# A written-out order of steps, changed: first roots on two engines, block weights and bias sooner, later units placed anew

## The chip, the cores and the metric

The kernel runs on one core of a Trainium2 chip. A core has a matrix engine (TensorE, PE in the profile, with its weight loads shown apart as PEld), a vector engine (VectorE, DVE), a scalar engine (ScalarE, ACT), GpSimd (POOL) and a queue engine for transfers (SyncE, SP). They run side by side, each through its own list of instructions in order, and wait for each other by counters (semaphores). The metric is the device time of one execution in microseconds (us); less is better.

## The reference

The input `x` has 2048 tokens of 512 numbers (bf16). Both halves start from the same layer norm, and their sum is added to `x`:

```python
xn = _layernorm(x, axis=-1)
return x + _A_ref(xn, A_wqkv, A_w_phi, A_wo) + _B_ref(xn, B_w1, B_b1, B_w2)
```

`_A_ref` is linear attention with 32 heads of 16: queries and keys are multiplied by a 16x16 matrix per head (`w_phi`), a softmax over the 16 is taken of the result and of its negative, and these 32 features replace the exponential kernel of attention:

```python
phi_k = jnp.concatenate([_softmax(pk, axis=-1), _softmax(-pk, axis=-1)], axis=-1)
kv = jnp.einsum("bhsf,bhsd->bhfd", phi_k, v)
num = jnp.einsum("bhqf,bhfd->bhqd", phi_q, kv)
den = jnp.einsum("bhqf,bhf->bhq", phi_q, z)[..., None] + 1e-6
```

`_B_ref` is a two-layer network with 1792 hidden units, a bias `b1` and the activation mish, `h * tanh(softplus(h))`.

## The kernel before, in words

The 2048 tokens are 16 tiles of 128, in four groups of four. The order of all the work is written out by hand in the string `STEPS` (line 24): one short name for one step, with its numbers, `@b` for the bank of PSUM (0 to 5) that it uses, and `a`, `v` or `p` for the engine that does it (ScalarE, VectorE, GpSimd). A loop at line 649 calls the functions in that order, and the table `run` (line 628) says which function a name stands for. There is no scheduler behind it: each engine gets its instructions in the order in which the steps stand. The waits between engines are put in by the framework, from which instruction reads or writes which buffer, in that same order.

The steps that matter here:

- `LS i`, `RS i`, `AZ i`, `TP i`, `TC i` (lines 550 to 589): moments of tile `i` of the first group, its root (one over the square root of variance plus epsilon), the centring, the transposition on TensorE (`ptr`), and the copy out of PSUM. `RS i a` is `Ln` and `Exp` on ScalarE (lines 558 and 559); `RS i p` is an addition and a power on GpSimd (lines 171 and 172).
- `TW`, `TK`, `WB`, `F0`, `FD`: key weights turned on TensorE (`ptw`), copied, multiplied by the block-diagonal matrix `Wbd` that `WB` makes of `w_phi` (`pfold`), and copied to `wkp`. `PB` and `CB` turn the bias and copy it to `b1f`. `KM` makes a mask that is used late.
- `LP i`: logits of the keys of the first two tiles (line 204). `L s i` and `LC s i`: logits of slot `s`, tile `i` (slots 0 to 3 are the keys of the four groups, 4 to 7 the queries), and their copy to SBUF by `take` (line 247). `V`, `VC`: values and their copy.
- `WL 1`, `WL 2` (`wide`, line 619): the logits of tiles 1 and 2 of the second group, not in a bank of the six but in a tile of two banks of their own, `pwide`, one half each. Their copies are `LC 1 1` and `LC 1 2`:

```python
wide_of[0] = ps2.tile([P, 2, 512], FP32, name="pwide", tag="kv")
pl_of[1, i] = project(wkp, TPG + i, wide_of[0][:, i - 1, :])
```

- `H u`, `M u`: a hidden unit, that is 128 hidden numbers for 512 tokens, as four matmuls (`ph`, line 223), and its mish on ScalarE (line 234), which also adds the bias.
- `E s`, `X s k`, `S s k`, `R s k`, `N s k`: the softmax of a slot: extremes on VectorE, exponentials on ScalarE (line 283), sums on VectorE (line 300), inverses and normalisation. `A`: the keys' products with the values.
- `LN g`, `AP g k`: layer norm of a later group, with a transposition by transfer. `DX`, `DW`, `WT`: loads on SP.
- From `KV` on: `W`, `Q`, `G`, `C` are the attention of the queries, `O` the second layer, `P` the projection, `Y` the residual and the store.

Mish and the exponentials need different tables on ScalarE. Whenever the kind of function changes, `table` (line 135) loads one (line 139).

Of the kernel before, what the change touches and what calls it, by code (L numbers as in the profile page):

```python
# [21 lines left out]

WARM, SHORT = 8, 0
STEPS = """
LS 0; LS 1; TW 0 @0; DX 2; TK 0 a; AW; TW 1 @1; RS 0 p; KM; WB; AZ 0; RS 1 p; AZ 1; F0 0 @2; TK 1 a;
FD 0 a; TP 0 @3; PB @4; TP 1 @5; TC 1 a; F0 1 @0; F0 2 @1; FD 2 a; TC 0 v; F0 3 @3; CB; FD 1 v; FD 3
a; LP i @4,2; LS 2; V 1 @5; LS 3; RS 2 a; AZ 2; TP 2 @0; RS 3 a; AZ 3; V 0 @1; LC 0 0 a; LC 0 1 a;
AM; TC 2 v; VC 1 a; TP 3 @3; TC 3 v; L 0 2 @4; LC 0 2 a; H 0 @0; M 0; L 0 3 @2; LC 0 3 a; LN 1; H 1
@3; E 0 0; M 1; H 2 @5; H 3 @4; H 4 @0; H 5 @2; M 2; M 3; M 4; AP 1 0; H 6 @3; AP 1 1; E 0 1; H 7
@5; LN 2; H 8 @4; H 9 @0; M 5; VC 0 a; M 6; M 7; H 10 @2; H 11 @1; H 12 @3; M 8; DX 3; WL 1; M 9; X  # L30
0 1; X 0 0; L 1 0 @5; L 1 3 @4; M 10; LC 1 0 v; LC 1 3 v; H 13 @0; H 14 @5; WL 2; M 11; M 12; M 13;
V 6 @4; LC 1 1 a; H 15 @2; H 16 @1; M 14; H 17 @3; H 18 @0; M 15; M 16; M 17; H 19 @5; M 18; M 19;
LN 3; S 0 1; LC 1 2 a; AP 2 0; AP 2 1; H 20 @2; H 21 @1; H 22 @3; M 20; M 21; M 22; H 23 @0; M 23;
VC 6 a; AP 3 0; AP 3 1; H 24 @5; M 24; H 25 @2; M 25; H 26 @1; H 27 @3; H 28 @0; M 26; H 29 @4; S 0
0; L 2 3 @5; M 27; M 28; M 29; E 1 0; L 2 0 @2; E 1 1; LC 2 0 v; L 2 2 @1; LC 2 2 v; L 3 2 @3; WT; R
0 0 a; LC 2 3 a; F 0 @0; L 2 1 @4; N 0 0; F 1 @2; F 2 @5; X 1 0; FC 2 a; L 3 0 @1; LC 3 0 a; FC 1 a;
LC 2 1 v; V 3 @4; FC 0 a; LC 3 2 v; V 4 @5; F 3 @3; FC 3 a; V 7 @1; V 2 @2; X 1 1; A 0 0; E 2 0; L 4
0 @0; VC 3 a; E 2 1; L 4 2 @3; L 3 1 @4; VC 2 a; R 0 1 a; VC 4 a; LC 4 0 a; S 1 1; N 0 1; L 3 3 @2;
L 4 3 @5; L 4 1 @0; VC 7 a; LC 3 3 a; LC 4 2 a; V 9 @1; LC 4 3 v; V 5 @2; S 1 0; X 2 0; VC 5 a; V 8
@3; R 1 1 a; VC 9 a; LC 3 1 a; N 1 1; VC 8 v; A 0 1; V 11 @5; VC 11 v; R 1 0 a; N 1 0; LC 4 1 a; H  # L40
30 @2; M 30; H 31 @1; M 31; H 32 @4; H 33 @3; H 34 @0; M 32; M 33; H 35 @5; M 34; M 35; H 36 @2; H
37 @1; H 38 @4; H 39 @3; M 36; M 37; M 38; M 39; DW 2; H 40 @0; H 41 @5; H 42 @2; E 3 0; M 40; M 41;
M 42; H 43 @1; A 1 0; S 2 0; M 43; A 1 1; DW 3; R 2 0 a; E 3 1; L 5 0 @4; X 2 1; L 6 2 @3; E 4 0; LC
5 0 a; L 5 3 @0; LC 5 3 a; E 4 1; V 14 @5; O 0 @2; VC 14 v; V 13 @1; X 3 0; X 3 1; V 10 @4; N 2 0;
VC 13 a; V 12 @5; VC 12 a; L 6 0 @0; VC 10 a; S 2 1; S 3 1; V 15 @1; R 2 1 a; N 2 1; L 6 1 @5; S 3
0; L 5 2 @4; LC 6 0 a; VC 15 a; X 4 0; LC 5 2 a; LC 6 2 a; O 1 @0; L 5 1 @1; LC 6 1 v; L 6 3 @4; H
44 @3; H 45 @5; S 4 0; A 2 0; R 3 0 a; N 3 0; LC 5 1 a; R 3 1 a; N 3 1; LC 6 3 a; H 46 @1; A 2 1; A
3 0; X 4 1; W 4 0 v; S 4 1; M 44; H 47 @4; M 45; A 3 1; M 46; M 47; H 48 @3; H 49 @5; M 48; H 50 @1;
H 51 @4; KV; M 49; W 4 1 v; M 50; E 5 0; E 5 1; M 51; H 52 @3; M 52; Q 0 0; G 0 0; H 53 @5; H 54 @1;
L 7 0 @4; Q 0 1; M 53; H 55 @3; L 7 3 @5; M 54; G 0 1; Q 1 0; O 2 @1; C 0 a; G 1 0; LC 7 0 a; LC 7 3  # L50
a; Q 1 1; L 7 1 @4; E 6 0; X 5 0; S 5 0; G 1 1; C 1 a; W 5 0 v; O 3 @5; LC 7 1 a; O 4 @4; E 6 1; M
55; P 0; Y 0; P 1; Y 1; O 5 @3; X 5 1; Q 2 0; P 2; L 7 2 @2; P 3; S 5 1; G 2 0; Q 2 1; Y 2; W 5 1 a;
O 6 @0; O 7 @1; LC 7 2 a; G 2 1; E 7 0; C 2 a; X 6 0; S 6 0; X 6 1; Y 3; W 6 0 a; Q 3 0; O 8 @2; P
4; G 3 0; Q 3 1; E 7 1; G 3 1; X 7 0; Y 4; P 5; O 9 @5; Q 4 0; S 6 1; O 10 @4; C 3 a; W 6 1 a; G 4
0; Q 4 1; G 4 1; Y 5; S 7 0; C 4 a; O 11 @3; X 7 1; W 7 0 v; Q 5 0; P 6; Y 6; P 7; G 5 0; S 7 1; Q 5
1; G 5 1; C 5 a; O 12 @0; W 7 1 a; Q 6 0; Y 7; P 8; P 9; Y 8; G 6 0; Q 6 1; O 13 @1; G 6 1; Q 7 0; G
7 0; P 10; P 11; Q 7 1; C 6 v; O 14 @2; Y 9; G 7 1; Y 10; P 12; P 13; OH 0 @5; Y 11; C 7 a; P 14; PH
0; OH 1 @4; Y 12; Y 13; Y 14; YH 0; PH 1; YH 1
"""


# [620 lines left out]
```

## Time and profile before

| | |
|---|---|
| median of 3 runs | 174.02 us (173.9 to 174.33) |
| profiled execution | 173.64 us, of it 171.9 us span from the first instruction to the last |
| PE busy | 167.7 us, 98% of the span |
| DVE busy | 142.2 us, 83% |
| ACT busy | 125.3 us, 73% |
| POOL busy | 7.8 us, 5% |
| mean granted TensorE clock | 0.998 |

The span leaves out 1.74 us of the profiled execution. The profile gives each engine's busy time, the chain of waits that ended last, groups of equal instructions by line, and a timeline: start and duration in us, engine, line, operation, what it writes and reads, how many alike were put together, and in brackets how long the engine had been idle and what ended that. Starts on one engine can lie up to 0.1 us ahead of the end of the instruction before, since they overlap. A matmul's duration includes its way through the array: those of 512 columns have 0.379 us in the profile and follow each other every 0.216 us (eight of them take 1.89 us).

### The profile page before, as it was taken

The page shows a single profiled execution, that of the slowest core. Times are in us where ns is not written, and L with a number is a line of the kernel's source. Part 1 is how long each engine was busy: PE and PEld are TensorE (multiplying, and loading weights), DVE is VectorE, ACT ScalarE, POOL GpSimd, SP SyncE. Part 2 cuts the span into 40 slices and gives each one's busy share as a digit, 9 for nine tenths or more (in the row PEclk, how much of TensorE's full clock was granted, in tenths as well). Part 3 has the DMA queues.
Part 4 walks back from the last instruction along what each step waited for, and adds up shares of the span by engine and source line. Part 5 has one row for each costly group of instructions (what it writes and reads, how often), then busy time and mean ns, then how long its engine had stood idle before and what let it go on. Part 6 is the DMA issues. An engine that isn't in the chain of part 4 may idle for free.

```text
span 171.9 us, 2729 instructions
## 1 busy us (share of the span) xinstructions
PE 167.7 (98%) x1044; PEld 82.4 (48%) x1044; DVE 142.2 (83%) x220; ACT 125.3 (73%) x204; POOL 7.8 (5%) x23
## 2 busy tenths in 40 slices
PE   8899999999999999999999999999999999999993
PEld 2554444444455454454444744544444444554452
DVE  2859998999599999989999998699789987875333
ACT  2788899988989899789897988996286275532200
POOL 4302102200000000000000000000000000000000
PEclk9999999999999999999999999999999999999999
DMA  5997280099960000000000254209345628768631
GB/s 139 273 377 256 43 203 0 2 183 209 302 225 0 0 4 0 0 0 4 0 0 0 59 99 91 56 7 156 92 113 104 149 58 192 153 135 199 155 96 61
DMA packets 44201, 18.02 MB, mean 105 GB/s; under 512 B 35996, under 2 KB 44188, under 8 KB 44188
## 3 DMA queue, kind: packets, MB, share of 16 engines
q1 hardware_dynamic: 43344, 17.60, 42.0%
q10 hardware_dynamic: 844, 0.25, 0.6%
q8 instruction: 8, 0.13, 0.3%
q14 instruction: 5, 0.04, 0.1%
HBM read 7.10 MB, written 2.10 MB: 53 GB/s over the span
## 4 chain that ended last, share of the span: by engine, by line
PE 95%; DMA 1%; POOL 1%; DVE 1%; issue 0%
PE po L457 28%; PE ph L223 28%; PE pl L189 14%; PE po L464 8%; PE pv L189 8%; PE pnd L412 2%; PE pkv L381 2%; DMA x_sb<-in_A_x_dram 1%; PE pl L204 1%; PE pwide L189 1%; PE pfold L151 1%; POOL rstd L172 1%; PE ptr L570 0%; DVE stats L165 0%; POOL rstd L171 0%
## 5 line engine op out<-in xcount | busy, mean ns | idle before, releaser
L457 PE MATMUL po<-w_sb,acts 128*128 128x512 bf16 (+2 forms) x238 | 50.8, 366 | 0.0
L223 PE MATMUL ph<-xnT,w_sb 128*128 128x512 bf16 x224 | 50.1, 379 | 0.0
L234 ACT ACTIVATE acts<-ph,b1f 128x512 bf16<-128x512 f32 x56 | 36.8, 694 | 4.7 <-PE ph L223 4.3
L300 DVE TENSOR_REDUCE s<-e 128x128 f32<-128x2048 bf16 x16 | 36.4, 2276 | 0.0
L457 PEld LDWEIGHTS <-acts 128*128 128x128 bf16 x238 | 22.2, 98 | 24.1
L223 PEld LDWEIGHTS <-w_sb 128*128 128x128 bf16 x224 | 21.6, 98 | 25.2
L283 ACT ACTIVATE e<-e 128x2048 bf16<-128x2048 bf16 x16 | 30.3, 1910 | 0.0
L189 PEld LDWEIGHTS <-xnT 128*128 128x128 bf16 x184 | 17.5, 98 | 19.6 <-DMA wv<-in_A_wqkv_dram 0.2
L471 DVE TENSOR_TENSOR x_sb<-po,x_sb 128x512 bf16<-128x512 f32 (+2 forms) x17 | 11.0, 656 | 8.8 <-PE po L464 8.8
L427 ACT COPY ds<-pnd 128x32 f32<-128x32 f32 x16 | 3.0, 185 | 18.3 <-PE pnd L412 18.3
L464 PE MATMUL po<-wqk,xnT 128*128 128x512 bf16 (+2 forms) x68 | 15.6, 366 | 0.0
L189 PE MATMUL pv<-wv,xnT 128*128 128x512 bf16 x64 | 15.4, 379 | 0.0
L189 PE MATMUL pl<-wqk,xnT 128*128 128x512 bf16 x64 | 15.4, 379 | 0.0
L247 ACT CAST p_sb<-pl 128x512 bf16<-128x512 f32 x22 | 12.3, 583 | 1.9 <-PE pl L189 1.9
L165 DVE BATCH_NORM_STATS2 stats<-x_sb 128x6 f32<-128x512 bf16 x16 | 10.1, 678 | 4.1 <-DMA x_sb<-in_A_x_dram 4.1
L139 ACT ACT_TABLE_LOAD x10 | 12.8, 1283 | 0.2
L258 DVE TENSOR_TENSOR m<-m 128x512 bf16<-128x512 bf16 (+1 forms) x32 | 11.5, 359 | 1.1
L189 PE MATMUL pl<-wkp,xnT 128*128 128x512 bf16 x48 | 11.5, 379 | 0.0
L258 DVE TENSOR_TENSOR m<-p_sb 128x1024 bf16<-128x1024 bf16 x16 | 10.9, 682 | 0.0
L267 DVE TENSOR_TENSOR e<-p_sb,m 128x2048 bf16<-128x2048 bf16 x8 | 9.8, 1225 | 0.9 <-PE pkv L381 0.7
L334 DVE TENSOR_TENSOR e<-e,r 128x2048 bf16<-128x2048 bf16 x8 | 9.7, 1218 | 0.7 <-ACT r L309 0.7
L267 DVE TENSOR_TENSOR e<-m,p_sb 128x2048 bf16<-128x2048 bf16 x8 | 9.8, 1225 | 0.3
(67 smaller groups left out, 133.5 us busy)
## 6 DMA issues: line engine op xcount, KB each, us to landing
w_sb<-in_B_w_dram SPq DMA_DIRECT2D x4, 896.0 KB, 7.3
out_dram<-x_sb SPq DMA_DIRECT2D x15, 128.0 KB, 2.0
x_sb<-in_A_x_dram SPq DMA_DIRECT2D x3, 512.0 KB, 7.8
wv<-in_A_wqkv_dram SPq DMA_DIRECT2D x1, 512.0 KB, 4.9
wqk<-in_A_wo_dram SPq DMA_DIRECT2D x1, 512.0 KB, 9.7
x_sb<-in_A_x_dram SPq DMA_DIRECT2D x2, 128.0 KB, 2.4
x_sb<-in_A_x_dram SPq DMA_DIRECT2D x1, 256.0 KB, 3.9
qT<-e SPq DMA_TRANSPOSE x16, 2.8
```

Source lines behind the costliest of these rows:

```text
L139: nc.scalar.preload_act_table_set(name)
L189: nc.tensor.matmul(pp, lhsT=xnT[:, t, kt, :], rhs=w[:, kt, :], start=(kt == 0), stop=(kt == KT - 1),)
L223: nc.tensor.matmul(ph_of[u][:], lhsT=w1_sb[:, kt, f * P : (f + 1) * P], rhs=xnT[:, g * TPG : (g + 1) * TPG, kt, :], start=(kt == 0), stop= ...
L234: nc.scalar.activation(acts[:, f, g * 512 : (g + 1) * 512], ph_of.pop(u)[:], ACT.Mish, bias=b1f[:, f : f + 1])
L247: copy(p_of[s][:, i, :], pl_of.pop((s, i)))
L258: nc.vector.tensor_tensor(out=m[:], in0=src[:, :, 0:half], in1=src[:, :, half : 2 * half], op=op)
L267: nc.vector.tensor_tensor(out=e_of[s][:].rearrange("p t j l c -> p (t j) l c")[:, :, pl, :].rearrange("p t (c e o) -> p t c e o", e=8, o=2 ...
L283: nc.scalar.activation(v, v, ACT.Exp)
L300: nc.vector.reduce_sum(t[:], pair(s, k).rearrange("p t j l (c e) -> p (t j l c) e", e=16), axis=AX.X)
L457: nc.tensor.matmul(po_of[t, c.stop][:, c], lhsT=acts[:, f, t * P : (t + 1) * P], rhs=w2_sb[:, f, c], start=(f == 0), stop=False,)
L464: nc.tensor.matmul(po_of[t, c.stop][:, c], lhsT=oT_of[t // 2][:, t % 2 * 4 + j, :], rhs=wo_sb[:, j, c], start=False, stop=(j == 3),)
L471: nc.vector.tensor_tensor(out=y, in0=po_of.pop((t, c.stop))[:, c], in1=y, op=ALU.add)
```

## The change

Only `STEPS` is changed; the steps are the same, in another order and with other banks and, for some copies, inverses and roots, on another engine. In the first group, `RS 0` goes from GpSimd to ScalarE and `RS 3` from ScalarE to GpSimd; `WB` and `PB` stand sooner, `KM` later. Behind that the order of nearly everything differs somewhat. The core of the diff, cut to the first half of the order:

```diff
-LS 0; LS 1; TW 0 @0; DX 2; TK 0 a; AW; TW 1 @1; RS 0 p; KM; WB; AZ 0; RS 1 p; AZ 1; F0 0 @2; TK 1 a;
-FD 0 a; TP 0 @3; PB @4; TP 1 @5; TC 1 a; F0 1 @0; F0 2 @1; FD 2 a; TC 0 v; F0 3 @3; CB; FD 1 v; FD 3
-a; LP i @4,2; LS 2; V 1 @5; LS 3; RS 2 a; AZ 2; TP 2 @0; RS 3 a; AZ 3; V 0 @1; LC 0 0 a; LC 0 1 a;
-AM; TC 2 v; VC 1 a; TP 3 @3; TC 3 v; L 0 2 @4; LC 0 2 a; H 0 @0; M 0; L 0 3 @2; LC 0 3 a; LN 1; H 1
-@3; E 0 0; M 1; H 2 @5; H 3 @4; H 4 @0; H 5 @2; M 2; M 3; M 4; AP 1 0; H 6 @3; AP 1 1; E 0 1; H 7
-@5; LN 2; H 8 @4; H 9 @0; M 5; VC 0 a; M 6; M 7; H 10 @2; H 11 @1; H 12 @3; M 8; DX 3; WL 1; M 9; X
-0 1; X 0 0; L 1 0 @5; L 1 3 @4; M 10; LC 1 0 v; LC 1 3 v; H 13 @0; H 14 @5; WL 2; M 11; M 12; M 13;
-V 6 @4; LC 1 1 a; H 15 @2; H 16 @1; M 14; H 17 @3; H 18 @0; M 15; M 16; M 17; H 19 @5; M 18; M 19;
-LN 3; S 0 1; LC 1 2 a; AP 2 0; AP 2 1; H 20 @2; H 21 @1; H 22 @3; M 20; M 21; M 22; H 23 @0; M 23;
...
+LS 0; LS 1; RS 0 a; TW 0 @0; RS 1 p; WB; AW; TW 1 @1; AZ 0; PB @2; TK 0 a; F0 0 @3; AZ 1; TK 1 a;
+CB; FD 0 a; TP 0 @4; TP 1 @5; F0 1 @0; F0 2 @2; TC 0 v; TC 1 a; KM; FD 2 a; F0 3 @1; FD 3 a; FD 1 v;
+LP i @4,3; LS 2; RS 2 a; LS 3; RS 3 p; V 1 @5; AM; AZ 2; TP 2 @0; TC 2 a; V 0 @2; LC 0 0 a; LC 0 1
+v; AZ 3; TP 3 @1; TC 3 v; L 0 2 @3; L 0 3 @0; LC 0 2 a; H 0 @4; LN 1; LC 0 3 a; DX 2; E 0 0; M 0; AP
+1 0; AP 1 1; VC 1 a; E 0 1; LN 2; H 1 @1; H 2 @3; M 1; M 2; H 3 @0; M 3; VC 0 a; H 4 @4; H 5 @5; H 6
+@1; M 4; H 7 @3; M 5; H 8 @0; H 9 @2; H 10 @4; H 11 @5; M 6; L 1 0 @1; M 7; M 8; M 9; X 0 0; X 0 1;
+H 12 @3; LC 1 0 v; L 1 3 @0; H 13 @2; LC 1 3 v; S 0 1; DX 3; M 10; M 11; M 12; LN 3; WL 1; AP 2 0; M
+13; LC 1 1 a; WL 2; LC 1 2 v; AP 2 1; H 14 @1; M 14; H 15 @0; M 15; H 16 @4; M 16; H 17 @5; M 17; H
+18 @3; H 19 @2; H 20 @1; H 21 @0; M 18; H 22 @4; M 19; M 20; M 21; M 22; H 23 @5; H 24 @3; H 25 @2;
...
```

What is left out moves in the same way: values, logits, softmax steps, second layer and stores in another order among themselves. Sixteen steps change engine in all: the two roots; from ScalarE to VectorE the copies `LC 0 1`, `LC 1 2`, `LC 4 3`, `LC 6 3`, `VC 5` and `VC 7`, the inverses `W 6 1` and `C 7`; from VectorE to ScalarE the copies `TC 2`, `LC 2 1`, `LC 2 2`, `LC 3 0`, `LC 3 2` and `LC 6 1`.

More of the change, by code (lines that the diff above doesn't have):

```diff
@@ L30 @@
-@5; LN 2; H 8 @4; H 9 @0; M 5; VC 0 a; M 6; M 7; H 10 @2; H 11 @1; H 12 @3; M 8; DX 3; WL 1; M 9; X
-0 1; X 0 0; L 1 0 @5; L 1 3 @4; M 10; LC 1 0 v; LC 1 3 v; H 13 @0; H 14 @5; WL 2; M 11; M 12; M 13;
-V 6 @4; LC 1 1 a; H 15 @2; H 16 @1; M 14; H 17 @3; H 18 @0; M 15; M 16; M 17; H 19 @5; M 18; M 19;
-LN 3; S 0 1; LC 1 2 a; AP 2 0; AP 2 1; H 20 @2; H 21 @1; H 22 @3; M 20; M 21; M 22; H 23 @0; M 23;
-VC 6 a; AP 3 0; AP 3 1; H 24 @5; M 24; H 25 @2; M 25; H 26 @1; H 27 @3; H 28 @0; M 26; H 29 @4; S 0
@@ L35 @@
[L35 to L58, printed above, removed]
+LS 0; LS 1; RS 0 a; TW 0 @0; RS 1 p; WB; AW; TW 1 @1; AZ 0; PB @2; TK 0 a; F0 0 @3; AZ 1; TK 1 a;
+CB; FD 0 a; TP 0 @4; TP 1 @5; F0 1 @0; F0 2 @2; TC 0 v; TC 1 a; KM; FD 2 a; F0 3 @1; FD 3 a; FD 1 v;
@@ new lines @@
+13; LC 1 1 a; WL 2; LC 1 2 v; AP 2 1; H 14 @1; M 14; H 15 @0; M 15; H 16 @4; M 16; H 17 @5; M 17; H
+18 @3; H 19 @2; H 20 @1; H 21 @0; M 18; H 22 @4; M 19; M 20; M 21; M 22; H 23 @5; H 24 @3; H 25 @2;
+H 26 @1; H 27 @0; H 28 @4; M 23; M 24; M 25; M 26; M 27; M 28; H 29 @5; M 29; AP 3 0; AP 3 1; S 0 0;
+WT; R 0 0 a; E 1 0; L 2 2 @3; L 2 0 @2; E 1 1; L 2 3 @1; LC 2 0 v; LC 2 3 a; LC 2 2 a; L 2 1 @0; LC
+2 1 a; N 0 0; V 6 @4; VC 6 a; F 0 @5; F 1 @2; FC 0 a; F 2 @1; FC 2 a; F 3 @3; L 3 0 @0; E 2 0; L 3 2
@@ new lines @@
+@4; FC 3 a; X 1 0; FC 1 a; V 4 @5; LC 3 0 v; LC 3 2 a; L 3 1 @1; A 0 0; V 7 @3; LC 3 1 a; V 3 @0; X
+1 1; E 2 1; VC 7 v; V 5 @2; V 9 @4; L 4 0 @1; VC 4 a; VC 9 a; L 4 3 @3; VC 3 a; LC 4 0 a; X 2 0; VC
+5 v; S 1 0; L 4 1 @5; LC 4 3 a; LC 4 1 a; L 4 2 @2; R 0 1 a; V 2 @4; L 3 3 @0; S 1 1; LC 3 3 a; V 8
+@1; LC 4 2 a; VC 2 a; R 1 1 a; S 2 0; R 1 0 a; N 0 1; VC 8 v; H 30 @3; H 31 @5; H 32 @0; H 33 @2; DW
+2; H 34 @4; M 30; M 31; M 32; H 35 @1; M 33; M 34; A 0 1; N 1 0; A 1 0; H 36 @3; H 37 @5; H 38 @0; H
@@ new lines @@
+39 @2; M 35; M 36; M 37; H 40 @4; H 41 @1; H 42 @3; H 43 @5; M 38; M 39; N 1 1; E 3 0; M 40; E 3 1;
+M 41; M 42; M 43; A 1 1; L 6 3 @0; L 5 3 @2; X 3 1; E 4 0; E 4 1; DW 3; L 6 0 @4; L 5 0 @1; LC 5 0
+a; LC 5 3 a; R 2 0 a; V 15 @3; VC 15 a; V 11 @5; V 13 @1; L 5 2 @2; VC 13 a; V 14 @3; S 3 1; X 2 1;
+VC 11 v; V 12 @1; LC 6 0 a; VC 12 a; LC 6 3 v; X 3 0; X 4 0; L 6 2 @5; L 6 1 @0; LC 6 2 a; LC 6 1 a;
+V 10 @4; N 2 0; S 2 1; VC 14 v; VC 10 a; S 3 0; O 0 @1; S 4 0; R 2 1 a; R 3 0 a; R 3 1 a; L 5 1 @3;
@@ new lines @@
+LC 5 1 a; N 2 1; LC 5 2 a; X 4 1; H 44 @5; O 1 @0; N 3 1; M 44; H 45 @4; H 46 @3; M 45; M 46; N 3 0;
+A 2 0; A 2 1; A 3 0; A 3 1; W 4 0 v; H 47 @2; M 47; H 48 @5; M 48; S 4 1; KV; H 49 @4; M 49; H 50
+@3; H 51 @2; H 52 @5; M 50; M 51; M 52; Q 0 0; W 4 1 v; G 0 0; E 5 0; H 53 @4; H 54 @3; Q 0 1; M 53;
+L 7 0 @2; M 54; L 7 1 @5; E 5 1; G 0 1; C 0 a; L 7 3 @4; LC 7 0 a; LC 7 3 a; Q 1 0; O 2 @3; LC 7 1
+a; L 7 2 @2; X 5 0; G 1 0; O 3 @4; X 5 1; H 55 @5; E 6 0; E 6 1; Q 1 1; S 5 0; LC 7 2 a; G 1 1; C 1
@@ new lines @@
+a; P 0; W 5 0 v; S 5 1; M 55; P 1; Y 0; O 4 @2; O 5 @5; P 2; X 6 0; Q 2 0; W 5 1 a; O 6 @1; G 2 0; Q
+2 1; G 2 1; Y 1; Y 2; S 6 0; O 7 @0; E 7 0; Q 3 0; C 2 a; W 6 0 a; G 3 0; P 3; Y 3; E 7 1; X 6 1; O
+8 @3; O 9 @4; Q 3 1; G 3 1; S 6 1; P 4; Y 4; C 3 a; P 5; W 6 1 v; Q 4 0; X 7 0; O 10 @2; Y 5; G 4 0;
+Q 4 1; S 7 0; G 4 1; O 11 @5; C 4 a; X 7 1; Q 5 0; G 5 0; P 6; W 7 0 v; P 7; Y 6; Q 5 1; G 5 1; O 12
+@1; Q 6 0; P 8; S 7 1; C 5 a; W 7 1 a; P 9; Y 7; Y 8; G 6 0; Q 6 1; G 6 1; C 6 v; O 13 @0; Q 7 0; Y
@@ L59 @@
+9; P 10; P 11; G 7 0; Q 7 1; G 7 1; C 7 v; O 14 @3; OH 0 @4; P 12; P 13; P 14; Y 10; Y 11; PH 0; OH
+1 @2; PH 1; Y 12; Y 13; Y 14; YH 0; YH 1
 """
```

## The prediction

> **What bounds the kernel now.** I read the page's first lines, then who waited for whom on PE, then the timeline of the start and of the stretch from 21 to 32 us.
>
> ```profile
> span 171.9 us, 2729 instructions
> ...
> PE 167.7 (98%) x1044; PEld 82.4 (48%) x1044; DVE 142.2 (83%) x220; ACT 125.3 (73%) x204; POOL 7.8 (5%) x23
> ...
> PE 95%; DMA 1%; POOL 1%; DVE 1%; issue 0%
> ```
>
> TensorE is busy for 98% of the span and is 95% of the chain that ended last. The view of PE's own waits has two lines in all:
>
> ```profile
> PE warm L515 <- PEq L666: 0.8, 1, 0.8
> PE ptr L570 <- DVE xn L176: 0.4, 1, 0.4
> ```
>
> So the last time PE waits for anybody is at `ptr` (step `TP 1`), at 6.55 us. From there to 169.2 us it has work without a break. Two things follow. What can be gained by order alone lies in front of 6.55 us. And whatever makes PE wait later is paid in full: no later wait of PE exists that could take it up.
>
> **The start, part by part.** In the timeline of the start, engine by engine (GpSimd, VectorE, PE, ScalarE):
>
> ```profile
> 4.13 0.23 POOL L171 TENSOR_SCALAR rstd<-mv 128x1 f32<-128x1 f32 x1 [1.54 <-DVE mv L167]
> 4.45 0.58 POOL L172 TENSOR_TENSOR rstd<-rstd,mhalf 128x1 f32<-128x1 f32 x1
> 5.01 0.36 POOL L171 TENSOR_SCALAR rstd<-mv 128x1 f32<-128x1 f32 x1
> 5.45 0.60 POOL L172 TENSOR_TENSOR rstd<-rstd,mhalf 128x1 f32<-128x1 f32 x1
> ```
>
> ```profile
> 3.86 0.18 DVE L167 BATCH_NORM_AGGREGATE mv<-stats 128x2 f32<-128x6 f32 x1
> ...
> 4.65 0.18 DVE L167 BATCH_NORM_AGGREGATE mv<-stats 128x2 f32<-128x6 f32 x1
> ...
> 6.08 0.41 DVE L176 TENSOR_SCALAR xn<-x_sb,mv,rstd 128x512 bf16<-128x512 bf16 x1 [0.48 <-POOL rstd L172]
> ```
>
> ```profile
> 6.55 0.40 PE L570 MATMUL ptr<-ident,xn 128*128 128x128 bf16 x4 [0.38 <-DVE xn L176]
> ```
>
> ```profile
> 8.81 0.29 ACT L558 ACTIVATE rstd<-mv,eps 128x1 f32<-128x1 f32 x1 [0.26 <-DVE mv L167]
> 9.14 0.20 ACT L559 ACTIVATE rstd<-rstd 128x1 f32<-128x1 f32 x1
> ```
>
> `RS 0` on ScalarE takes 0.29 + 0.20 us instead of 0.23 + 0.58, but tile 0 isn't what PE waits for; tile 1 is. Its moments are there at 4.65 + 0.18 = 4.83, and its root starts at 5.01 because GpSimd still works on tile 0. With GpSimd free it starts 0.09 after the moments, as the first root did (4.04 to 4.13), at 4.92: 0.09 sooner, and 0.13 more if its addition takes 0.23 as for tile 0 and not 0.36. `TP 1` gains 0.09 to 0.22 us; I take 0.15. That is the whole gain of the edit, 0.09% of the time.
>
> The other edits of the start I cost at nothing. `WB` loses `KM` ahead of it on VectorE. `TK 0` on ScalarE gets `RS 0` ahead of it, 0.5 us from about 4.13, while ScalarE waits for the first `ptw` anyway. `PB` ahead of `F0 0` is one small matmul that waits for the bias; PE has 0.38 us of idle time ahead of `TP 1` (row at 6.55) that hides it. `RS 3` on GpSimd (0.23 + 0.58 against 0.29 + 0.20) and the table load of `AM`, now ahead of `TC 2`, take some tenths of a microsecond from tiles that PE wants at 10 to 11 us. If that cover goes, PE is some tenths late there, but the next part swallows it: PE will have 4 us to spare.
>
> **The step that decides: `WL 2` behind `LC 1 1`.** Both halves of `pwide` are one tile. Before, the order is `WL 1`, `WL 2`, `LC 1 1`, `LC 1 2`; after, it is `WL 1`, `LC 1 1`, `WL 2`, `LC 1 2`. The framework orders by tile: in the built program the first matmul of `WL 2` now waits for ScalarE's counter, for just the value that the copy `LC 1 1` brings it to. Before, no matmul of `pwide` waits for another engine. So PE stands at `WL 2` until ScalarE has copied `WL 1`'s half. When is that? PE, then ScalarE, in the timeline before:
>
> ```profile
> 24.37 1.03 PE L189 MATMUL pwide<-wkp,xnT 128*128 128x512 bf16 x4
> 25.23 1.89 PE L189 MATMUL pl<-wkp,xnT 128*128 128x512 bf16 x8
> 26.96 1.89 PE L223 MATMUL ph<-xnT,w_sb 128*128 128x512 bf16 x8
> 28.68 1.03 PE L189 MATMUL pwide<-wkp,xnT 128*128 128x512 bf16 x4
> 29.55 1.03 PE L189 MATMUL pv<-wv,xnT 128*128 128x512 bf16 x4
> ```
>
> ```profile
> 21.98 0.69 ACT L234 ACTIVATE acts<-ph,b1f 128x512 bf16<-128x512 f32 x1 [0.18 <-PE ph L223]
> 22.68 1.28 ACT L139 ACT_TABLE_LOAD   x1
> 23.98 3.71 ACT L283 ACTIVATE e<-e 128x2048 bf16<-128x2048 bf16 x2
> 27.71 1.28 ACT L139 ACT_TABLE_LOAD   x1
> 29.00 2.42 ACT L234 ACTIVATE acts<-ph,b1f 128x512 bf16<-128x512 f32 x4
> 31.30 0.60 ACT L247 CAST p_sb<-pwide 128x512 bf16<-128x512 f32 x1
> ```
>
> ScalarE's order up to `LC 1 1` is the same after the change: ten mishes (`M 0` to `M 9`), a table load, two exponentials, a table load, four mishes (`M 10` to `M 13`), then the copy. `M 9` waits for PE's `H 9`, ahead of which PE has the same matmuls as before, so all of it moves by PE's 0.15 at most (the exponentials need `E 0 1`, which ends well ahead, below). The copy ends at 31.90 - 0.15 = 31.75, and PE goes on about 0.06 later, the handover from VectorE's `xn` (6.49) to `ptr` (6.55): at 31.81.
>
> ```profile
> 21.76 1.23 DVE L267 TENSOR_TENSOR e<-m,p_sb 128x2048 bf16<-128x2048 bf16 x1
> ```
>
> PE gets to `WL 2` sooner than before: `H 14` stands behind it now, and four matmuls of 512 columns take 29.55 - 28.68 = 0.87 us from start to start. The same point of PE's work was at 28.68 - 0.87 = 27.81. So PE idles from about 27.66 to 31.81, and all behind it is 31.81 - 27.81 = 4.00 us later than before. Bounds: with none of the 0.15 it is 4.15; with all of the 0.22, 3.93. ScalarE can't be much sooner, since from 22.68 to 31.90 it has no idle time in these rows.
>
> While PE stands, no other engine needs it much. VectorE goes on with sums and layer norms; `LC 1 2` and what it has behind that wait some 3 us, and VectorE has 17% of the span to spare. The units placed anew behind this (values, logits, softmax, second layer; six copies each way between ScalarE and VectorE, and `W 6 1` and `C 7` on VectorE) I cost at nothing: PE's matmuls are the same 1044, and the other engines come out of the gap with a lead of 4 us that the old order didn't have. If one of them were still late, the price would be of the size of PE's one such wait here, 0.4 us. The tail keeps its shape: `OH 1`, `PH 1`, `YH 1`, one store.
>
> **The clock.** A stop of 4 us may cost more than its length. The start shows a slow state of PE, and the end shows how fast it comes back:
>
> ```profile
> 0.83 3.41 PE L515 MATMUL warm<-const-bfloat16-1.0 128*128 128x512 bf16 x8 [0.83 <-PEq L666]
> 4.07 0.39 PE L577 MATMUL ptw<-ident,wkp 128*128 128x128 bf16 x4
> ...
> 168.78 0.39 PE L464 MATMUL po<-wqk,xnT 128*128 128x128 bf16 x4
> ```
>
> ```profile
> 167.78:171.19 3.41, 1.38 (x21) 1.09 (x18) 1.27 (x3) 0.00 (x0) 0.00 (x0) 1.00 0.25 77
> 169.20:171.10 1.90, 0.00 (x0) 0.00 (x0) 0.29 (x1) 0.00 (x0) 0.00 (x0) 1.00 0.40 124
> 171.20:171.90 0.70, 0.00 (x0) 0.00 (x0) 0.00 (x0) 0.00 (x0) 0.00 (x0) 0.50 0.00 0
> ```
>
> The first eight matmuls of 512 columns take 3.41 us, the eight of `pl` above 1.89: half speed. By 4.07 PE is at full speed, after 3.24 us of work at most. The second fence has stretches of time with each engine's busy time, then the granted clock, DMA share and GB/s: PE's last matmul ends at 169.17, and the granted clock is 1.00 up to 171.1 and 0.50 from 171.2. So 2.0 us without a matmul were enough to halve it. A stop of 4.1 us is twice that. If PE comes back at half speed for about the 3.1 us that it took at the start (0.83 to about 3.94), it does 1.55 us of work in them and loses 1.55. Bounds: 0, if the clock stays, and about 3.1, if a first stretch at half speed doesn't count as busy and a second follows. I take 1.55, as the row at the end is nearest to what happens here.
>
> [...]
>
> **The sum.** 173.64 + 4.00 + 1.55 = 179.19 us against the profiled execution, which lies 0.38 under the median of the runs shown (174.02); that much I leave in the range. I say 179.2.
>
> **The rivals.**
> 1. The clock stays up through the stop. For it: nothing in the trace has PE idle for 4 us and then working again. Against it: the drop at the end. Time: 173.64 + 4.00 = 177.6.
> 2. The stop sets PE back by two stretches at half speed, or the stop itself is longer, because `LC 1 1` is later than I think. For it: the length of a second stretch isn't shown anywhere. Time: 173.64 + 4.00 + 3.1 = 180.7.
> 3. Not slower: the wait at `WL 2` is met before PE gets there, and only the start's gain is left: 173.64 - 0.15 = 173.5. That needs `LC 1 1` to end by 27.7, 4.1 us sooner than ScalarE did. For it: ScalarE waits for PE now and then ahead of 22 us (0.18 us in the row at 21.98). Against it: even without them the table load, two exponentials, table load, four mishes and copy are 9.2 us in a row, and they follow `M 9`, which follows `H 9`.
>
> **How the numbers follow.** Forecast (stop and one stretch at half speed): 0.70. First rival: 0.18. Second: 0.08. Third: 0.03; 0.01 for something else that is faster. A change of 0.3% (0.5 us) is about what a measurement of this kernel can tell from none. Slower than that: 0.96; same: 0.03, as the third rival's 0.15 us is 0.09%; faster: 0.01. The range goes from the first rival, 173.64 + 3.93 = 177.6 less 0.3 of scatter as the runs shown have, to the second, 180.7, so that only part of the second case and the third lie outside.
>
> **What would show it.** Right: in PE's waits a line for `pwide` behind ScalarE's `p_sb` (L247) of about 4.1 us, one time, and the chain of waits going through ScalarE's exponentials and table loads there; in the row of PE by slices a dent at 27 to 32 us; after it a stretch with a granted clock of 0.5 and 512-column matmuls 0.43 us apart; `ptr` of tile 1 at about 6.4 instead of 6.55, with roots on ACT and POOL side by side; no other wait of PE behind 32 us. Wrong: no wait at `pwide`, or the stop there and a span longer by much more than it and the slow stretch, which would mean that a unit placed anew is late further on.

## The result and the profile after

The changed kernel took 180.12 us (median, 179.48 to 180.39) beside 174.33 us for the kernel before (173.9 to 174.54) on the same chip: a ratio of 1.0333, with a 95% interval of 1.0307 to 1.0358. It is 3.3% slower. A ratio leaves out an execution that took over 1.5% longer than the fastest of the same kernel; below, that is one execution of the second experiment. The profiled execution took 179.97 us, of it 178.2 us span.

The page of the changed kernel, cut to the rows that answer those of before: the busy times, PE's row by slices and the granted clock by slices, and the chain that ended last:

```profile
span 178.2 us, 2716 instructions
...
PE 168.7 (95%) x1029; PEld 82.6 (46%) x1044; DVE 143.8 (81%) x223; ACT 124.9 (70%) x200; POOL 8.0 (4%) x23
...
PE   8889994799999999999999999999999999999993
...
PEclk9999999699999999999999999999999999999999
...
PE 87%; ACT 6%; DMA 3%; SPq 2%; issue 1%; DVE 0%
```

PE's busy time is nearly the same, 168.7 us for 167.7, but it has a dent in slices seven and eight (27 to 36 us; a slice is 4.5 us), and the granted clock has its own in slice eight. ScalarE, which had no part in the printed chain of before, now holds 6% of it. Who waited for whom on PE:

```profile
PE pwide L189 <- ACT p_sb L247: 4.0, 1, 4.0
PE warm L515 <- PEq L666: 0.8, 1, 0.8
PE pv L189 <- DMA wv<-in_A_wqkv_dram: 0.6, 1, 0.6
PE ptw L577 <- DMA wkp<-in_A_wqkv_dram: 0.6, 1, 0.6
```

The first line is new: one wait of 4.0 us of the second half of `pwide` (step `WL 2`) for the copy of the first (`LC 1 1`). The timeline there, PE and then ScalarE:

```profile
27.52 1.03 PE L189 MATMUL pwide<-wkp,xnT 128*128 128x512 bf16 x4
32.51 1.87 PE L189 MATMUL pwide<-wkp,xnT 128*128 128x512 bf16 x4 [3.96 <-ACT p_sb L247]
34.17 6.18 PE L223 MATMUL ph<-xnT,w_sb 128*128 128x512 bf16 x24
```

```profile
23.25 1.28 ACT L139 ACT_TABLE_LOAD   x1
24.54 3.71 ACT L283 ACTIVATE e<-e 128x2048 bf16<-128x2048 bf16 x2
28.27 1.28 ACT L139 ACT_TABLE_LOAD   x1
29.56 2.42 ACT L234 ACTIVATE acts<-ph,b1f 128x512 bf16<-128x512 f32 x4
31.86 0.60 ACT L247 CAST p_sb<-pwide 128x512 bf16<-128x512 f32 x1
```

The copy ends at 32.46, and 0.05 us later PE goes on, but slowly: the four matmuls take 1.87 us instead of 1.03. The same in stretches of time (length, PE busy and matmuls, granted clock, DMA share, GB/s):

```profile
24.07:28.55 4.48, 4.43 (x20) 1.00 0.42 115
28.55:32.50 3.95, 0.00 (x0) 0.99 0.00 0
32.50:35.80 3.30, 3.29 (x8) 0.50 0.24 46
35.90:39.30 3.40, 3.40 (x17) 1.00 0.85 157
```

Eight matmuls in the 3.3 us after the stop, 17 in the 3.4 us behind: half speed, for one stretch that ends at 35.9. From there on PE has no wait, as before. The last two lines of PE's waits, 0.6 us each, belong to the start; the loads landed later in this execution. In the last experiment below, the same kernel again, the line of `pv` is gone and that of `ptw` is 0.4; the profiles of the filled and of the two shortened stops, which have the same start, show neither. So the two lines aren't the change's doing.

### The profile page after: what moved, and what is told of

Its sections match the earlier page's. It is cut to its first block, busy times and chain, and to the rows that moved or that the text cites. A ratio compares the mean times of both kernels' runs of the same rounds, so it can differ in the third digit from the quotient of the medians.

```text
span 178.2 us, 2716 instructions
## 1 busy us (share of the span) xinstructions
PE 168.7 (95%) x1029; PEld 82.6 (46%) x1044; DVE 143.8 (81%) x223; ACT 124.9 (70%) x200; POOL 8.0 (4%) x23
## 4 chain that ended last, share of the span: by engine, by line
PE 87%; ACT 6%; DMA 3%; SPq 2%; issue 1%; DVE 0%
PE po L457 27%; PE ph L223 26%; PE pl L189 12%; PE pv L189 8%; PE po L464 8%; DMA wv<-in_A_wqkv_dram 3%; PE pnd L412 2%; PE pkv L381 2%; ACT e L283 2%; ACT acts L234 2%; ACT L139 1%; PE pwide L189 1%; SPq L483 1%; PE pfold L151 1%; SPq L478 0%
## 5 line engine op out<-in xcount | busy, mean ns | idle before, releaser
L223 PE MATMUL ph<-xnT,w_sb 128*128 128x512 bf16 x224 | 51.0, 383 | 0.0
L234 ACT ACTIVATE acts<-ph,b1f 128x512 bf16<-128x512 f32 x56 | 37.4, 689 | 11.2 <-PE ph L223 11.0
L189 PE MATMUL pl<-wqk,xnT 128*128 128x512 bf16 x62 | 14.7, 379 | 0.1
L464 PE MATMUL po<-wqk,xnT 128*128 128x512 bf16 (+2 forms) x64 | 14.4, 365 | 0.2
L247 ACT CAST p_sb<-pl 128x512 bf16<-128x512 f32 x24 | 13.1, 595 | 1.4 <-PE pl L189 1.3
```

Of the source, the lines that this page charges most:

```text
L189: nc.tensor.matmul(pp, lhsT=xnT[:, t, kt, :], rhs=w[:, kt, :], start=(kt == 0), stop=(kt == KT - 1),)
L223: nc.tensor.matmul(ph_of[u][:], lhsT=w1_sb[:, kt, f * P : (f + 1) * P], rhs=xnT[:, g * TPG : (g + 1) * TPG, kt, :], start=(kt == 0), stop= ...
L234: nc.scalar.activation(acts[:, f, g * 512 : (g + 1) * 512], ph_of.pop(u)[:], ACT.Mish, bias=b1f[:, f : f + 1])
L247: copy(p_of[s][:, i, :], pl_of.pop((s, i)))
L464: nc.tensor.matmul(po_of[t, c.stop][:, c], lhsT=oT_of[t // 2][:, t % 2 * 4 + j, :], rhs=wo_sb[:, j, c], start=False, stop=(j == 3),)
```

## The experiments

My theory: the loss is the wait of `WL 2` for `LC 1 1`, 4 us, and one stretch at half clock that the stop brings about. The rivals: units placed anew elsewhere, or the start, carry a part; the clock has no part. A finer question came up on the way: how long a stop halves the clock. The first four kernels ran beside the kernel before at 173.80 us, the last three at 173.68 us.

**The wait alone taken away from the changed kernel.**

```diff
-LC 1 1 a; WL 2; LC 1 2 v;
+WL 2; LC 1 1 a; LC 1 2 v;
```

> The changed kernel with one swap: the second half of the wide tile is computed ahead of the copy of the first half, as before the change. Every engine has its instructions in exactly the same order as in the changed kernel; only the wait of that matmul goes. If the wait and the clock behind it are the whole loss, the time comes back to that of the kernel before: 174.2 us, between 173.7 and 174.8, with the mean granted clock at 0.998 again and no wait of PE behind 12 us. If units placed anew further on, or the roots of the start, carry a part of the loss, it stays above 175 us.

Measured: 173.68 us (173.44 to 174.16, 12 executions), a ratio of 0.9985 to the kernel before, interval 0.9971 to 0.9999. The whole loss is gone with one swap of two steps that leaves every engine's instructions in the same order. PE's work at that place is in one piece again, while ScalarE copies the first half at 31.31, long after both halves:

```profile
26.97 1.89 PE L189 MATMUL pwide<-wkp,xnT 128*128 128x512 bf16 x8
28.70 5.56 PE L223 MATMUL ph<-xnT,w_sb 128*128 128x512 bf16 x25
```

```profile
31.31 0.60 ACT L247 CAST p_sb<-pwide 128x512 bf16<-128x512 f32 x1
```

The rest of the change, all the other moves together, is worth 0.15% at the median, with an interval that just leaves out nothing: it costs no time, and whether it gains any is at the edge of what these times can tell.

**The wait alone put into the kernel before.**

```diff
-WL 2; M 11; M 12; M 13; V 6 @4; LC 1 1 a;
+M 11; M 12; M 13; LC 1 1 a; WL 2; V 6 @4;
```

> The kernel before with one edit: the copy of the first half of the wide tile stands ahead of the second half's matmuls. ScalarE's copy ended at 31.90 us there and PE was at the second half at 28.68, so PE stops for about 3.3 us. If the wait alone costs that, 174.2 + 3.3 = 177.5 us; if the clock is halved for one stretch behind it, 179.1 us. If the loss of the change came from elsewhere, the time stays under 176 us.

Measured: a ratio of 1.0194, interval 1.015 to 1.0239. The single executions differ by more than usual: 176.84 and 177.03 us with a mean clock of 1.00, 178.59 us with 0.99, and 180.15 us with 0.98, the one that the ratio leaves out. The profile is that of the 177.03 us. PE's wait there, and the stretches in the stop and behind it:

```profile
PE pwide L189 <- ACT p_sb L247: 3.1, 1, 3.1
```

```profile
28.90:32.00 3.10, 0.04 (x1) 1.00 0.00 0
32.04:35.40 3.36, 3.36 (x16) 1.00 0.25 47
```

The wait costs its length in a kernel that has nothing else of the change: the mean of the two executions with a clock of 1.00, 176.94 us, less 173.80 is 3.1 us. So the clock stayed up in two executions of four after a stop of over 3 us. The third lies 1.65 us above them, which fits one stretch at half speed; no trace shows it, and none shows what the fourth, 3.2 us above, consists of. The price of the clock was not the same in all executions of this one kernel.

**The stop filled.** Sixteen matmuls on constants, whose results nobody reads, stand in PE's order between the copy's place and `WL 2`.

```diff
-LC 1 1 a; WL 2;
+LC 1 1 a; DU 16 @1; WL 2;
...
+    def filler(n, b):
+        w = bank(b, "fill")
+        for _ in range(n):
+            nc.tensor.matmul(
+                w[:], lhsT=nc.const_aps.tensor(1.0, [P, P], BF16),
+                rhs=nc.const_aps.tensor(1.0, [P, 512], BF16), start=True, stop=True,
+            )
```

> The changed kernel with sixteen matmuls of 512 columns on constants, whose results nobody reads, between the two halves of the wide tile: 16 x 0.216 = 3.5 us of work in a stop of 4.0 us. The wait stays, and the second half starts at the same time. If the drop of the clock is worth 1.6 us, it goes: 180.1 - 1.6 = 178.5 us, and the granted clock stays at 1.0 after the stop. If the 4 us of the wait and something else are the whole loss, the time stays at 180.1 us.

Measured: 177.75 us (177.57 to 178.22), ratio 1.0219, interval 1.0188 to 1.0249. The second half of `pwide` still waits for the copy, but starts at full speed:

```profile
28.03 3.66 PE L631 MATMUL fill<-const-bfloat16-1.0 128*128 128x512 bf16 x16
31.75 1.02 PE L189 MATMUL pwide<-wkp,xnT 128*128 128x512 bf16 x4
```

```profile
28.03:31.70 3.67, 3.66 (x17) 1.00 0.00 0
31.75:35.20 3.45, 3.45 (x16) 1.00 0.28 53
```

It starts at 31.75, for 31.98 in the repetition below, because this execution was sooner from the start: its first matmuls of the values began at 9.05, those of the repetition at 9.26. So work that does nothing made the kernel faster than the changed one, 177.75 against 179.46 us (the repetition): 1.71 us, the price of the clock. The two were measured beside different executions of the kernel before; with each taken against its own (3.95 and 5.78 us above) the price is 1.83. What is left against the version without the wait, 177.75 - 173.68 = 4.07 us, is the stop.

**The stop shortened: the copy ahead of the four mishes.**

```diff
-M 10; M 11; M 12; LN 3; WL 1; AP 2 0; M 13; LC 1 1 a; WL 2;
+WL 1; AM; LC 1 1 a; M 10; M 11; M 12; LN 3; AP 2 0; M 13; WL 2;
```

> The changed kernel with the copy of the first half placed right behind the second table load, ahead of the four mishes. The copy then ends some 2.3 us sooner and PE's stop shrinks from 4.0 to about 1.8 us. Without a drop of the clock: 174.2 + 1.8 = 176.0 us. With a drop as after a stop of 4 us: 177.7 us. [...]

Measured: 175.93 us (175.55 to 176.28, four executions, all at a clock of 1.00 to two digits), ratio 1.0104, interval 1.0076 to 1.0133. The wait is down to 1.65 us, and the clock stays. The median lies 2.1 us above the kernel before, 0.5 more than the wait. Of these, 0.379 - 0.216 = 0.16 us come of counting idle time from the end of the last matmul, which is that much later than the next could have started; for the rest the trace shows no cause. PE's wait and the stretch behind it:

```profile
29.73 1.02 PE L189 MATMUL pwide<-wkp,xnT 128*128 128x512 bf16 x4 [1.65 <-ACT p_sb L247]
```

```profile
29.73:33.10 3.37, 3.37 (x16) 1.00 0.00 0
```

**The stop of middle length: the copy behind two of the four mishes.**

```diff
-M 10; M 11; M 12; LN 3; WL 1; AP 2 0; M 13; LC 1 1 a; WL 2;
+M 10; M 11; WL 1; LC 1 1 a; M 12; LN 3; AP 2 0; M 13; WL 2;
```

> The changed kernel with the copy of the first half behind two of the four mishes: PE's stop is 4.0 - 2 x 0.58 = 2.85 us, shorter than 3.4. Base 173.7 (the wait taken away): 176.5 us where the clock stays, 178.2 where it is halved for one stretch of 3.4 us, 179.9 for two. [...]

Measured: 176.62 us, ratio 1.0186, interval 1.0155 to 1.0216, in two groups: four executions at 176.39 to 176.66 us with a clock of 1.00, and two at 178.11 and 178.28 us with 0.99. The groups lie 1.65 us apart, which one stretch at half speed explains, and the lower lies 2.9 us above the version without the wait, which is the stop. The profile is of one with the drop:

```profile
30.59 1.05 PE L189 MATMUL pwide<-wkp,xnT 128*128 128x512 bf16 x4 [2.81 <-ACT p_sb L247]
31.45 4.87 PE L223 MATMUL ph<-xnT,w_sb 128*128 128x512 bf16 x14
```

```profile
28.04:31.40 3.36, 0.81 (x4) 1.00 0.00 0
31.50:34.80 3.30, 3.30 (x9) 0.50 0.16 31
34.90:38.30 3.40, 3.40 (x17) 1.00 1.08 179
```

PE goes on at 30.59 at full speed for four matmuls, and only then, at 31.5, does the clock halve: the drop comes after the stop, when PE works again. With a stop of 2.8 us the clock fell in two executions of six, and in four it stayed up.

**The start's root alone, in the kernel before.**

```diff
-LS 0; LS 1; TW 0 @0; ... RS 0 p; KM;
+LS 0; LS 1; RS 0 a; TW 0 @0; ... KM;
```

> The kernel before with one edit: the first tile's root goes to ScalarE, so that the second's has GpSimd to itself. The second tile is centred 0.09 to 0.22 us sooner, and its transposition starts at about 6.4 instead of 6.55. If that reaches the end: 173.8 - 0.15 = 173.65 us. If PE meets the load of the value weights instead, which lands at about 9.1 us and which PE reached only 0.15 to 0.3 us later, the gain stops there: 173.8, no difference.

Measured: 173.98 us, ratio 1.0005, interval 0.9987 to 1.0024: no difference. The transposition does start sooner, at 6.43:

```profile
6.43 0.40 PE L570 MATMUL ptr<-ident,xn 128*128 128x128 bf16 x4 [0.20 <-DVE xn L176]
```

What could stop the gain next are the weight loads of the values, which wait for their transfer: for 0.2 us here and in the kernel before alike, and for 0.4 us in the version without the wait (the view of PE's weight loads' waits, this kernel's line and then that version's):

```profile
PEld L189 <- DMA wv<-in_A_wqkv_dram: 0.2, 1, 0.2
```

```profile
PEld L189 <- DMA wv<-in_A_wqkv_dram: 0.4, 1, 0.4
```

In this profile the gain gets past them. The first matmuls of the values, this kernel's line and then that of the kernel before:

```profile
9.12 1.03 PE L189 MATMUL pv<-wv,xnT 128*128 128x512 bf16 x4
```

```profile
9.24 1.03 PE L189 MATMUL pv<-wv,xnT 128*128 128x512 bf16 x4
```

The 0.12 us are still there at the end of the span (171.80 us for 171.92). In the version without the wait they were lost: PE had the first group's `ptr` at 6.47 instead of 6.55, and its first matmuls of the values at 9.25. So a gain of a tenth of a microsecond can reach the end or be taken up by the transfer, and the medians cannot tell it from none: the interval of this run reaches from 0.2 us faster to 0.4 us slower.

**The change again.**

> The changed kernel as it is, beside the others on one chip. Stop of 4.0 us, then one stretch at half speed: 173.7 + 4.1 + 1.7 = 179.5 us. [...]

Measured: 179.46 us (179.42 to 179.68), ratio 1.0337, interval 1.0323 to 1.035. All four executions have a clock of 0.99, as had all five of the first result: after a stop of 4 us the clock fell every time. The stop is in the same place with the same length, but half a microsecond sooner than in the first profile, and `pv` has no line among PE's waits:

```profile
26.98 1.03 PE L189 MATMUL pwide<-wkp,xnT 128*128 128x512 bf16 x4
31.98 1.32 PE L189 MATMUL pwide<-wkp,xnT 128*128 128x512 bf16 x4 [3.97 <-ACT p_sb L247]
33.09 4.19 PE L223 MATMUL ph<-xnT,w_sb 128*128 128x512 bf16 x12
```

So the late loads of the values in the first profile are scatter between executions, and not part of the change.

## Why the prediction was right

**The wait** (predicted: PE idle from 27.66 to 31.81, all behind it 4.00 us later). It came where it was put. PE stopped for 3.96 and 3.97 us in the two profiles, counted from the end of the last matmul, 0.16 us later than the prediction counts; 4.07 us is what the time keeps when the clock is held up by filling. The swap that takes the wait away takes the whole loss away. The row that carried this step was ScalarE's, a line of work without idle time from the first table load to the copy, 9.22 us before and 9.21 after. (Ahead of it ScalarE's order is not quite the same, as the prediction has it: `LC 0 1` left it and `TC 2` came to it.) The swap was to be read in the order of two steps, and the price in the profile of another engine.

**The clock** (predicted: half speed for about 3.1 us, 1.55 us lost). The drop came, and the size was a little off: the stretch is 3.41 us (32.44 to 35.85 in the first profile), of which half is 1.7, and it costs 1.71 to 1.83 us by the filled stop and 1.65 by the two groups. That 3.1 us read from the start came so near was partly luck. In another execution PE stayed slow there for longer: in the profile of the shortened stop the first `pfold`, four matmuls at 5.73 us, still took 0.61 us, where the kernel before had 0.38 us at 5.33. Of the bounds, the lower one, 0, is what two executions of the kernel before with the wait show; no profile shows the upper one, two stretches, and no run shows whether a stretch at half speed counts as busy.

That the price would be paid in full here was argued from the 2.0 us without a matmul at the end. It was paid nine times of nine, but the argument was too simple: with stops of 2.8 and 3.1 us the clock stayed up in four executions of six and in two of four. What tells such stops apart no run shows directly. My estimate is in the last section; by it a stop of 4.0 us leaves about 2 us in one stretch of 3.41 us at the least.

**The start** (predicted: 0.09 to 0.22 us, 0.15 taken). The second tile was centred sooner by just that, in the first profile of the changed kernel:

```profile
5.93 0.41 DVE L176 TENSOR_SCALAR xn<-x_sb,mv,rstd 128x512 bf16<-128x512 bf16 x1 [0.47 <-POOL rstd L172]
```

5.93 instead of 6.08. But the sum let the 0.15 run on to ScalarE's copy and so to the end, without asking what is late next. In both profiles of the changed kernel it was lost on the way: the key weights landed late (`ptw`, 0.6 and 0.4 us), in the first the value weights too (`pv`, 0.6 us), and ScalarE's copy ended at 32.46 and at 31.92 for the 31.75 of the prediction. In the one profile of the kernel before with the root alone it is there at the end. The times can't tell the term from nothing, and the result doesn't depend on it.

**The rest at nothing.** The other moves together came out at -0.15%, with an interval that just leaves out zero. PE waits for no engine behind the stop, in any of the profiles. In the list of moves two copies are exchanged: in the diff `LC 3 0` goes from ScalarE to VectorE and `LC 4 3` from VectorE to ScalarE, so that it is still six each way, and the sum stays as it is.

**The sum.** 179.19 us against 180.12 in the first result and 179.46 in the second. The kernel before moved by as much between the two, from 174.33 to 173.68. Against it the change costs 5.79 and 5.78 us, where the sum has 4.00 + 1.55 = 5.55: the stop, with the start's gain already taken off it, was 0.07 short (4.07), the clock 0.16 short (1.71).

**The rivals.** A clock that stays up (177.6) is the 177.75 of the filled stop, which shows that the size was right and the condition not met. Two stretches at half speed (180.7) came in neither profile of the changed kernel, and its nine clocks are all 0.99, as one stretch gives. The third, that the wait is met in time, fell with the first profile; by its row ScalarE's copy would have had to end 4.2 us sooner, not 4.1.

## What to carry to other kernels

Where one buffer holds two results, as `pwide` does here, the framework's waits can go by the buffer as a whole and by the order in which the steps are written: the reader of the first half, written ahead of the writer of the second, made the second wait, though they touch different numbers. In an order written by hand, keep all writers of a shared buffer ahead of its first reader, or look which instruction of the bounding engine got a new wait; the price stands in the row of the engine that it waits for. And count for a stop of the matrix engine not only its length: here the clock stayed up with stops of 1.65 us in all four executions, it fell with those of 2.8 us in two of six (1.65 us more) and of 3.1 us in two of four (1.65 and 3.2 us more), and with those of 4.0 us in all nine (1.71 us by the filled stop).

## What the runs showed of the hardware

In the profile of the stop of middle length the clock fell at 31.5, 0.9 us after PE had begun again at 30.59. At the end of the changed kernel PE's last matmul ends at 175.5, and the clock holds for at least 3.6 us more, where in the kernel before it held for 2.0 us:

```profile
175.90:179.10 3.20, 0.00 (x0) 1.00 0.14 41
179.30:180.00 0.70, 0.00 (x0) 0.50 0.00 0
```

In the first profile of the changed kernel the clock changes at 5.13, 32.44, 35.85 and 179.21 us, that is 27.31, 3.41 and 143.36 us apart: 8, 1 and 42 steps of 3.413 us. From these distances I estimate where steps without a change of the clock lie; no trace marks them. Counted back in such steps from a drop in the same profile, the stretches that hold a stop or the end of the work are these (the kernel before with the wait, two; the copy ahead of the mishes; the end of the filled kernel; the changed kernel again):

```profile
26.97:30.38 3.41, 1.97 (x10) 1.00 0.00 0
30.38:33.79 3.41, 1.75 (x9) 1.00 0.00 0
```

```profile
27.22:30.63 3.41, 1.76 (x9) 1.00 0.00 0
```

```profile
171.67:175.08 3.41, 1.42 (x21) 1.00 0.38 120
```

```profile
29.15:32.56 3.41, 0.58 (x3) 1.00 0.00 0
```

The first three have 1.75 us of matmuls or more in 3.41, and the clock stayed up behind them; the last two have 1.42 and 0.58, and it fell as they ended. So it did behind the 0.81 us of the stop of middle length above, and at the end of the kernel before, behind the stretch from 167.78 to 171.19 with 1.38, and in the first profile of the changed kernel behind the one from 29.03 to 32.44 with none. So in these eight stretches it fell behind 1.99 us or more without matmuls, and stayed up behind 1.66 or less. By the same estimate equal stops differ from execution to execution by how they lie to the steps: the stop of 3.1 us lies on both sides of 30.38, with 1.44 and 1.66 us, and cost no more than its length; of the 2.8 us, 2.55 lie in one stretch. The executions without a profile can't be placed in this way.
